# Attention of later blocks: two 64-row chunks in nine visits inside y, instead of one chunk in 17 visits between h and y

## The chip, the cores and the metric

The kernel runs on one core of a Trainium2 chip. The metric is the device time of one execution in microseconds (us), of which the median over several runs is given. TensorE (PE) multiplies, VectorE (DVE), ScalarE (ACT) and GpSimd (POOL) work element by element, and SyncE (SP) issues the DMAs, which are the loads and stores between the chip's main memory and the on-chip buffers. Each engine executes its own instructions in order, and waits at an instruction until what it needs is there.

## The reference

A linear attention with decay works on blocks of 64 rows and carries a 64x64 state for each of 2 x 8 heads over the 12 blocks of a sequence. Its output goes through two MLPs, one after the other.

```python
# q, k, v: (2, 8, 768, 64); lam: (8,), between 0.97 and 0.99
for b in range(12):
    qb, kb, vb = the 64 rows of block b
    intra = (qb @ kb.T * Dmask) @ vb            # Dmask[i, j] = lam ** (i - j) for i >= j
    inter = (qb * lam ** (pos + 1)) @ kv_state
    out[block b] = intra + inter
    kv_state = lam ** 64 * kv_state + (kb * lam ** (63 - pos)).T @ vb
x = out as (1536, 512)
h = x @ w_in;  g = where(h > 0, h, exp(min(h, 0)) - 1);  x = g @ w_out      # 512 -> 2048 -> 512
h = x @ w_in2; g = P(h) / Q(h), a cubic over 1 + |b0 h| + |b1| h * h;  y = g @ w_out2
```

## The kernel before

The 1536 tokens are three blocks t of T = 512. Each MLP layer takes a block in NF = 16 steps f of 128 hidden units: `mlp_h` is the product x @ w_in of step f, 12 matmuls of 512 columns (line 435), and `mlp_y` adds g @ w_out into four accumulating banks, 12 matmuls (line 517, and line 426 for a block's last y). There are 12 since every operand is split into a high and a low part in a narrower float type, and three of the four products are computed for each of four tiles. y runs LAG = 2 steps behind h. Between them stand, for each step, relu and exp on ScalarE (lines 448 and 449), max on VectorE (line 450, which frees h's bank), the high part ghi on ScalarE (line 452) and the low part glo on VectorE (line 453).

A first stage computes the attention of token block 0 in chunks of 128. The attention of blocks 1 and 2 is done in 64-row chunks, numbered 8 to 23, by `att_visit` in the steps of t = 0 and t = 1 of layer 0 (step s = 16 t + f). A visit stands between h and y of its step. On TensorE it has up to four matmuls of 64 x 64 for each of four pairs of heads, in two quadrants each: the scores k · q of a chunk n (line 340), and for the chunk d of the visit before scores · v (line 345), the state's product k · v (line 351) and state · q (line 356). Around them stand the fade of q by powers of lam on POOL (line 371), the mask on VectorE (line 376), the copy of d's outputs `sm_out` on ScalarE (line 384), the decay of the keys, `sm_decay_k`, on ScalarE (line 365), and the state: addition on VectorE (line 388), decay on ScalarE (line 395). The first visit also makes the powers of lam for 64 rows by four matmuls (line 333).

The order on each engine is written out by hand here (`manual_schedule`): what the program issues first stands first in an engine's queue. SP's queue is in program order through the whole kernel. It carries the loads of raw weights (lines 114 and 122), of k and q (`qk`, line 308, two DMAs) and of k and v (`kv`, line 323, four DMAs a chunk). Raw weights come as 64-bit numbers, of which VectorE makes 32-bit ones by three integer instructions (lines 78, 81 and 84); their high half is then made on ScalarE (line 127) and the low half on VectorE (line 128). During t = 1 `park_w2` does the same for half of the second layer's weights and stores them. The visits of before are at the steps f given here, for t = 0 and t = 1:

```python
visits = [(3, 5, 7, 9, 10, 12, 13, 14, 15), (2, 4, 6, 8, 10, 12, 14, 15)]
```

Of the kernel before, what the change touches and what calls it, by code (L numbers as in the profile page):

```python
# [8 lines left out]
F32 = mybir.dt.float32  # L9
# [3 lines left out]
ALU = mybir.AluOpType  # L13
# [16 lines left out]
def fused_kernel(ctx, tc, lam, qkv, w1, w2, ab, out):  # L30
# [16 lines left out]
    ph = ctx.enter_context(tc.tile_pool(name="ph", bufs=2, space=PSUM))  # L47
# [252 lines left out]
    aa_tiles = []  # L300

    def sm_load_qk(k):
# [10 lines left out]
        for b in range(2):  # L313
            chunk[k + b] = {"q": qk[:, :, 0, b * CS:(b + 1) * CS],
                            "k": qk[:, :, 1, (1 - b) * CS:(2 - b) * CS]}

    def sm_load_kv(k):
        c, b, row = k // 2, k % 2, 4 * P
        chunk[k]["kv"] = kv = qq.tile([P, NP, 2, D], F32, tag="kv", name=f"kv{k}")
# [7 lines left out]
    def sm_products(n, d):  # L327

        if not aa_tiles:
            aa_tiles.extend(pa.tile([P, T], F32, tag=f"pa{i}", name=f"aa{i}")  # L330
                            .rearrange("p (x m i) -> p x m i", x=2, m=NP) for i in range(2))
            for r in ROWS:
                nc.tensor.matmul(aa_tiles[1][r, 1], lhsT=pick[r], rhs=mask64[r, :, 1:CS + 1],  # L333
                                 start=True, stop=True, skip_group_check=True)
            nc.scalar.activation(out=qpow[:, :, 0:CS], in_=aa_tiles[1][:, 1], func=AF.Copy)
        pn, pd = chunk.get(n), chunk.get(d)
        for m in range(NP):
            if pn:
                for r in ROWS:
                    nc.tensor.matmul(aa_tiles[0][r, 0, m], lhsT=pn["k"][r, m],  # L340
                                     rhs=pn["q"][r, m], start=True, stop=True,
                                     skip_group_check=True)
            if pd:
                for i, r in enumerate(ROWS):
                    nc.tensor.matmul(aa_tiles[1][ROWS[1 - i], 0, m], lhsT=pd["kv"][r, m, 1],  # L345
                                     rhs=pd["s"][r, m], start=m == 0, stop=d % KB == 0,
                                     skip_group_check=True)
        for m in range(NP):
            if pd and d % KB < KB - 1:
                for r in ROWS:  # L350
                    nc.tensor.matmul(aa_tiles[0][r, 1, m], lhsT=pd["kv"][r, m, 0],  # L351
                                     rhs=pd["kv"][r, m, 1], start=True, stop=True,
                                     skip_group_check=True)
            if pd and d % KB:
                for i, r in enumerate(ROWS):
                    nc.tensor.matmul(aa_tiles[1][ROWS[1 - i], 0, m], lhsT=state[r, m, 0],  # L356
                                     rhs=pd["q"][r, m], start=False, stop=True,
                                     skip_group_check=True)

    def sm_decay_k(n):  # L360

        kv = chunk[n]["kv"]
        if n % KB < KB - 1:
            for m in range(NP):
                nc.scalar.activation(out=kv[:, m, 0], in_=kv[:, m, 0], func=AF.Copy,
                                     scale=mask64[:, m, CS - 1:CS])

    def sm_decay_q(n):
        q = chunk[n]["q"]
        if n % KB:  # L370
            nc.gpsimd.tensor_tensor(out=q, in0=q, in1=qpow[:, :, 0:CS], op=ALU.mult)

    def sm_mask(n):
        b = chunk[n]
        b["s"] = s = ap_.tile([P, NP, CS], F32, tag="s", name=f"s{n}")
        nc.vector.tensor_tensor(out=s, in0=aa_tiles[0][:, 0], in1=mask64[:, :, 0:CS], op=ALU.mult)

    def sm_out(d):

        t, js = d * CS // T, slice(d * CS % T, d * CS % T + CS)  # L380
        if t not in xraw:
            xraw[t] = xr.tile([P, NP, T], F32, tag="xr", name=f"xr{t}")
        first, last = d % KB == 0, d % KB == KB - 1
        nc.scalar.activation(out=xraw[t][:, :, js], in_=aa_tiles[1][:, 0], func=AF.Copy)
        if first:
            nc.scalar.activation(out=state[:, :, 0], in_=aa_tiles[0][:, 1], func=AF.Copy)
        elif not last:
            nc.vector.tensor_tensor(out=state[:, :, 0], in0=aa_tiles[0][:, 1],
                                    in1=state[:, :, 1], op=ALU.add)

    def sm_decay_state(d):

        if d % KB not in (0, KB - 1):
            for m in range(NP):
                nc.scalar.activation(out=state[:, m, 1], in_=state[:, m, 0], func=AF.Copy,
                                     scale=qpow[:, m, CS - 1:CS])

# [102 lines left out]
    def mlp_y(layer, t, f):  # L500
# [27 lines left out]
    with ExitStack() as actx:  # L528
# [4 lines left out]
        qq = actx.enter_context(tc.tile_pool(name="qq", bufs=2))  # L533

# [20 lines left out]
        dmask = ac.tile([P, H, C + 1], F32, name="dmask")  # L555
        qpow = ac.tile([P, NP, C], F32, name="qpow")
        state = ac.tile([P, NP, 2, D], F32, name="state")

        mask64 = dmask.rearrange("p (m h) i -> p m h i", h=2)[:, :, 1, CS:]
# [19 lines left out]
        yy, hh = ((py, "y"),) * 2, ((ph, "h"),) * 2  # L579
# [323 lines left out]
```

## Time and profile before

| | |
|---|---|
| median of 3 runs (lowest to highest) | 571.95 us (571.62 to 572.47) |
| profiled execution | 572.56 us |
| its span, first to last instruction | 570.8 us |
| mean granted TensorE clock | 0.999 |
| TensorE busy | 564.6 us, 99% of the span |
| VectorE busy | 464.7 us, 81% |
| ScalarE busy | 358.5 us, 63% |
| GpSimd busy | 29.8 us, 5% |
| DMA traffic | 64.58 MB, 113 GB/s in the mean |

Busy time is the time in which an engine works on an instruction; matmuls overlap one another, so TensorE's is no measure of its efficiency. The span leaves out what lies around the program; the profiled execution's own time holds it. All rows further down are from this one execution, and their times count from the span's start.

### The profile page before, as it was taken

What the parts mean: (1) busy time and instruction counts of PE and PEld (TensorE: products, weight loads), DVE (VectorE), ACT (ScalarE), POOL (GpSimd) and SP (SyncE); (2) the same over time, 40 slices, a digit from 0 to 9 for tenths busy, and PEclk for the clock granted to TensorE, in tenths of its full rate; (3) what the DMA queues carried; (4) which work ended last, traced back from release to release, by engine and by line L of the source; (5) the groups of instructions that cost most, each with busy time, mean ns of one, the idle gap of its engine ahead of it and who ended that gap; (6) DMA issues with size and microseconds to landing.
All of it is one profiled execution on the core that took longest, in us unless ns stands there. A gap on an engine that the chain in (4) does not pass through costs nothing.

```text
span 570.8 us, 9255 instructions
## 1 busy us (share of the span) xinstructions
PE 564.6 (99%) x3550; PEld 464.9 (81%) x3550; DVE 464.7 (81%) x722; ACT 358.5 (63%) x690; POOL 29.8 (5%) x51
## 2 busy tenths in 40 slices
PE   8999999999999999999999999999999999999997
PEld 7877888888888888888888888888888888888885
DVE  6999999965676635877979999888898888898882
ACT  3746646875554545555568976667877666776672
POOL 7401001100100000000000000000000000000000
PEclk9999999999999999999999999999999999999999
DMA  8977677464687513434432500000400000200001
GB/s 291 318 225 243 237 227 214 107 206 128 204 240 229 165 49 136 167 135 177 150 108 78 182 3 1 1 2 0 145 3 2 0 1 0 75 0 1 1 1 74
DMA packets 41215, 64.58 MB, mean 113 GB/s; under 512 B 20178, under 2 KB 20178, under 8 KB 41170
## 3 DMA queue, kind: packets, MB, share of 16 engines
q1 hardware_dynamic: 41168, 63.98, 35.8%
q8 instruction: 28, 0.46, 0.3%
q14 instruction: 17, 0.14, 0.1%
q10 hardware_dynamic: 2, 0.00, 0.0%
HBM read 53.48 MB, written 10.49 MB: 112 GB/s over the span
## 4 chain that ended last, share of the span: by engine, by line
PE 98%; DMA 1%; SPq 0%; ACT 0%; issue 0%
PE h L435 46%; PE y L517 43%; PE y L426 3%; PE aa L340 1%; DMA att<-qkv_in 1%; PE aa L351 1%; PE pa L243 1%; PE pa L209 1%; PE pa L249 0%; PE aa L356 0%; PE aa L345 0%; SPq L192 0%; PE sums L256 0%; PE pa L291 0%; ACT o L487 0%; PE aa L333 0%
## 5 line engine op out<-in xcount | busy, mean ns | idle before, releaser
L435 PE MATMUL h<-xhi,w 128*128 128x512 f32 x768 | 204.8, 389 | 0.0
L517 PE MATMUL y<-ghi,w 128*128 128x512 f32 x712 | 191.8, 392 | 0.0
L435 PEld LDWEIGHTS h<-xhi,w 128*128 128x128 f32 x768 | 143.8, 188 | 30.3 <-DVE w L128 0.4
L517 PEld LDWEIGHTS y<-ghi,w 128*128 128x128 f32 x712 | 132.3, 188 | 27.8
L435 PE MATMUL h<-xlo,w 128*128 128x512 f32 x384 | 102.6, 389 | 0.0
L517 PE MATMUL y<-glo,w 128*128 128x512 f32 x356 | 95.3, 389 | 0.0
L435 PEld LDWEIGHTS h<-xlo,w 128*128 128x128 f32 x384 | 72.1, 188 | 15.0
L517 PEld LDWEIGHTS y<-glo,w 128*128 128x128 f32 x356 | 66.8, 188 | 14.2
L461 ACT ACTIVATE a<-h,babs 128x512 f32<-128x512 f32 x48 | 33.0, 688 | 63.8 <-PE h L435 63.8
L448 ACT ACTIVATE a<-h 128x512 f32<-128x512 f32 x48 | 28.3, 589 | 43.1 <-PE h L435 42.9
L465 DVE SCALAR_TENSOR_TENSOR b<-b,babs,a 128x512 f32<-128x512 f32 x48 | 36.0, 751 | 20.9 <-ACT b L462 20.7
L450 DVE SCALAR_TENSOR_TENSOR b<-a,h 128x512 f32<-128x512 f32 x48 | 32.7, 681 | 15.3 <-ACT a L449 12.1
L452 ACT ACTIVATE ghi<-b 128x512 fp32r<-128x512 f32 x48 | 30.0, 626 | 22.4 <-DVE b L450 22.4
L453 DVE TENSOR_TENSOR glo<-b,ghi 128x512 fp32r<-128x512 f32 x48 | 34.0, 709 | 7.0 <-ACT ghi L452 4.8
L463 ACT ACTIVATE p<-h,cab 128x512 f32<-128x512 f32 x48 | 37.7, 785 | 0.0
L467 ACT ACTIVATE a<-b,one 128x512 f32<-128x512 f32 x48 | 35.0, 729 | 3.1 <-DVE b L465 2.6
L469 DVE SCALAR_TENSOR_TENSOR p<-p,cab,h 128x512 f32<-128x512 f32 x48 | 35.8, 746 | 1.2
L473 DVE SCALAR_TENSOR_TENSOR b<-b,one,a 128x512 f32<-128x512 f32 x48 | 35.8, 746 | 0.1
L475 DVE SCALAR_TENSOR_TENSOR p<-p,cab,a 128x512 f32<-128x512 f32 x48 | 35.8, 746 | 0.0
L58 DVE TENSOR_TENSOR glo<-p,ghi 128x512 fp32r<-128x512 f32 x48 | 33.0, 688 | 3.0 <-PE y L426 1.5
L468 DVE TENSOR_TENSOR p<-p,h 128x512 f32<-128x512 f32 x48 | 32.8, 682 | 2.9 <-ACT p L463 2.9
L477 DVE SCALAR_TENSOR_TENSOR p<-b,p 128x512 f32<-128x512 f32 x48 | 33.1, 690 | 1.2
(88 smaller groups left out, 611.2 us busy)
## 6 DMA issues: line engine op xcount, KB each, us to landing
raw<-w_in SPq DMA_DIRECT2D x64, 512.0 KB, 4.5
att<-qkv_in SPq DMA_DIRECT2D x16, 256.0 KB, 6.0
qk<-qkv_in SPq DMA_DIRECT2D x16, 256.0 KB, 4.3
kv<-qkv_in SPq DMA_DIRECT2D x64, 64.0 KB, 4.0
w2d<-wbuf SPq DMA_DIRECT2D x16, 256.0 KB, 4.5
wbuf<-w2d SPq DMA_DIRECT2D x16, 256.0 KB, 2.8
x2d<-o SPq DMA_DIRECT2D x12, 256.0 KB, 2.3
x2r<-x2d SPq DMA_DIRECT2D x12, 256.0 KB, 3.1
```

The source lines that it names most:

```text
L58: lo_eng.tensor_tensor(out=lo, in0=src, in1=hi.bitcast(F32), op=ALU.subtract)
L435: nc.tensor.matmul(h, lhsT=w[:, a, 0, k * P:(k + 1) * P], rhs=xs[layer, t, k][b], start=i == k == 0, stop=i == 2 and k == NP - 1)
L453: lambda: nc.vector.tensor_tensor(out=glo, in0=b, in1=ghi.bitcast(F32), op=ALU.subtract)]
L461: nc.scalar.activation(out=a, in_=h, func=AF.Abs, scale=babs[:, 0:1])
L463: nc.scalar.activation(out=p, in_=h, func=AF.Identity, scale=cab[:, 3:4], bias=cab[:, 2:3])
L465: nc.vector.scalar_tensor_tensor(out=b, in0=b, scalar=babs[:, 1:2], in1=a, op0=ALU.mult, op1=ALU.add)
L467: nc.scalar.activation(out=a, in_=b, func=AF.Ln, bias=one[:, 0:1])
L469: nc.vector.scalar_tensor_tensor(out=p, in0=p, scalar=cab[:, 1:2], in1=h, op0=ALU.add, op1=ALU.mult)
L473: nc.vector.scalar_tensor_tensor(out=b, in0=b, scalar=one[:, 0:1], in1=a, op0=ALU.add, op1=ALU.mult)
L475: nc.vector.scalar_tensor_tensor(out=p, in0=p, scalar=cab[:, 0:1], in1=a, op0=ALU.add, op1=ALU.mult)
L477: nc.vector.scalar_tensor_tensor(out=p, in0=b, scalar=2.0, in1=p, op0=ALU.subtract, op1=ALU.mult, reverse0=True)
L517: nc.tensor.matmul(ys[layer, t][m], lhsT=w[:, a, 1, m * P:(m + 1) * P], rhs=g[b], start=f == i == 0, stop=False)
```

## The change

Two chunks are handled in one visit, and there are nine visits instead of 17, at the steps `at = [3, 6, 9, 11, 14, 18, 22, 26, 30]`. A visit stands inside the y of its step, behind the seventh of its twelve matmuls. Its outputs go to the bank of h that is free at that time, so the two banks of h have fixed names, h0 and h1, and take turns with the step. The scores of both chunks share one bank (aa1), the state's products another (aa0); the state has three parts instead of two. The keys of a visit are decayed in the step before it, state additions and decays are in the two steps behind it. The ten DMAs of a pair (kv of an odd chunk, qk, kv of the next chunk) are issued together, at the end of the step of the visit before. The tables of masks and powers for 64 rows are made in the first stage; those for 128 rows lie in a weight's place. `load_raw(2)` is called in step 8 instead of step 3. In the steps with a visit the last of the instructions on weights is issued behind the visit.

```diff
+    def sm_products(n, d, spare):
+        if d is not None:
+            aa_x[0] = spare.rearrange("p (m x i) -> p m x i", x=2, m=NP)
+        for j in range(2):
+            pn = chunk.get(n + j) if n is not None else None
+            pd = chunk.get(d + j) if d is not None else None
+            for m in range(NP):
+                if pn: ...   # scores of n + j into aa_tiles[1][r, j, m]
+                if pd: ...   # scores . v of d + j into aa_x[0][., m, j]
+        for j in range(2):
+            c = n + j - 1 if n is not None else None
+            kv = chunk[c]["kv"] if c in chunk and c % KB < KB - 1 else None
+            pd = chunk.get(d + j) if d is not None and (d + j) % KB else None
+            for m in range(NP):
+                if kv is not None: ...   # k . v of chunk c into aa_tiles[0][r, j, m]
+                if pd: ...   # state j . q of d + j into aa_x[0][., m, j]
...
     def sm_decay_q(n):
-        q = chunk[n]["q"]
-        if n % KB:
-            nc.gpsimd.tensor_tensor(out=q, in0=q, in1=qpow[:, :, 0:CS], op=ALU.mult)
+        q = chunk[n]["qk"][:, :, 0].rearrange("p m (b i) -> p m b i", b=2)
+        nc.gpsimd.tensor_tensor(
+            out=q, in0=q, in1=pow64.rearrange("p m (b i) -> p m b i", b=1)
+            .to_broadcast([P, NP, 2, CS]), op=ALU.mult)
...
-    def mlp_y(layer, t, f):
+    def mlp_y(layer, t, f, between=None):
...
+                if between and (i, m) == (1, 2):
+                    between()
...
+        at = [3, 6, 9, 11, 14, NF + 2, NF + 6, NF + 10, NF + 14]
+        pairs = list(range(first, end, 2))
+        loads = {}
+        for i, k in enumerate(pairs[1:]):
+            for j, load in enumerate(((sm_load_kv, k - 1), (sm_load_qk, k), (sm_load_kv, k))):
+                loads.setdefault(at[i] if i else 1 + j, []).append(load)
+        loads.setdefault(at[-2], []).append((sm_load_kv, end - 1))
+        work, late, states = {}, {}, {}
+        for v, s in enumerate(at[:-1]):
+            k = first + 2 * v
+            if v:
+                late.setdefault(s - 1, []).extend((sm_decay_k, n) for n in (k - 1, k))
+            work.setdefault(s + 1, []).append((sm_decay_state, k))
+            states[s + 1] = k + 1
+            work.setdefault(s + 2 + (s + 2 == NF), []).append((sm_decay_state, k + 1))
...
+        def att_visit(s, f):
+            v = at.index(s)
+            spare = ph.tile([P, T], F32, tag=f"h{(f + 1) % 2}", name=f"ax{s}") if v else None
+            n = pairs[v] if v < len(pairs) else None
+            d = pairs[v - 1] if v else None
+            sm_products(n, d, spare)
+            if d is not None:
+                sm_out(d)
             if n is not None:
                 sm_mask(n)
                 sm_decay_q(n)
...
-                if t == 0 and f == 3:
+                if t == 0 and f == 8:
                     load_raw(2)
+                if len(queue) > LAG:
+                    mlp_y(*queue.pop(0), between=(lambda: att_visit(s, f)) if s in at else None)
+                if s in at:
+                    for w in now:
+                        run(w, 1)
                 lows = [op for w in now for op in w]
-                if len(queue) > LAG:
-                    mlp_y(*queue.pop(0))
+                for load, k in loads.get(s, ()):
+                    load(k)
```

ScalarE's queue in steps 10 and 11 of before, from the exp of step 10 to the high halves of step 11's weights; `a_0_10` is step 10's buffer, `kv_1051` a chunk's keys and values, `xr` the block's attention outputs, `ghi_0_10` the high part of g:

```order
L449 ACTIVATE a_0_10_1083<-a_0_10_1083 128x512
L384 ACTIVATE xr_763<-aa_613 128x4x64
L365 ACTIVATE kv_1051<-kv_1051,dmask 128x64 x4
L127 ACTIVATE w_10_1088<-wbuf 128x512 x2
L452 ACTIVATE ghi_0_10_1081<-b_0_10_1084 128x512
L448 ACTIVATE a_0_11_1170<-h_0_11_1155 128x512
L449 ACTIVATE a_0_11_1170<-a_0_11_1170 128x512
L127 ACTIVATE w_11_1182<-wbuf 128x1024
```

The same place in the changed kernel, where line 375 is the decay of the keys, 405 and 414 are the state's copy and its decay, and line 397 is `sm_out` of the visit at step 11:

```order
L467 ACTIVATE a_0_10_1143<-a_0_10_1143 128x512
L405 ACTIVATE state<-aa_462 128x4x64
L375 ACTIVATE kv_1115<-kv_1115,mask_162 128x64 x4
L375 ACTIVATE kv_1123<-kv_1123,mask_162 128x64 x4
L127 ACTIVATE w_10_1148<-wbuf 128x512 x2
L470 ACTIVATE ghi_0_10_1141<-b_0_10_1144 128x512
L414 ACTIVATE state<-state,pow_163 128x64 x4
L466 ACTIVATE a_0_11_1200<-h_0_11_1185 128x512
L467 ACTIVATE a_0_11_1200<-a_0_11_1200 128x512
L397 ACTIVATE xr_884<-ax_1226 128x4x128
L127 ACTIVATE w_11_1293<-wbuf 128x1024
```

Two chunks' keys stand there instead of one, ahead of the weights, and `sm_out` has moved behind step 11's exp.

SP's queue of before from the raw weights of step 9 to those of step 13 (`raw_12` are the raw weights of step 12, `kv` and `qk` chunks):

```order
L122 DMA raw_9_911<-w_in 128x1024 x2
L323 DMA kv_914<-qkv_in 64x4x64 x4
L308 DMA qk_919<-qkv_in 64x2x512 x2
L122 DMA raw_11_967<-w_in 128x1024 x2
L122 DMA raw_12_1048<-w_in 128x1024 x2
L323 DMA kv_1051<-qkv_in 64x4x64 x4
L114 DMA raw_14_1_1131<-w_in 128x1024
L114 DMA raw_15_1_1133<-w_in 128x1024
L323 DMA kv_1135<-qkv_in 64x4x64 x4
L308 DMA qk_1140<-qkv_in 64x2x512 x2
L122 DMA raw_13_1184<-w_in 128x1024 x2
```

And in the changed kernel:

```order
L122 DMA raw_9_943<-w_in 128x1024 x2
L122 DMA raw_11_991<-w_in 128x1024 x2
L114 DMA raw_12_0_994<-w_in 128x1024
L114 DMA raw_10_1_996<-w_in 128x1024
L122 DMA raw_12_1038<-w_in 128x1024 x2
L323 DMA kv_1115<-qkv_in 64x4x64 x4
L308 DMA qk_1120<-qkv_in 64x2x512 x2
L323 DMA kv_1123<-qkv_in 64x4x64 x4
L114 DMA raw_14_1_1169<-w_in 128x1024
L114 DMA raw_15_1_1171<-w_in 128x1024
L122 DMA raw_13_1216<-w_in 128x1024 x2
```

The loads of the pair for the visit at step 11 stand in one group behind the raw weights of step 12; `raw_12_0` and `raw_10_1` are the raw halves that moved to step 8.

VectorE's queue at the end of t = 1 in before; `b_1_15` is the max of the last step of the block, `xlo_2` the third block's low part, `raw_0_0` the first raw half of the second layer:

```order
L450 SCALAR_TENSOR_TENSOR b_1_14_2479<-a_1_14_2478,h_1_14_2463 128x512
L453 TENSOR_TENSOR glo_1_14_2477<-b_1_14_2479,ghi_1_14_2476 128x512
L58 TENSOR_TENSOR xlo_2_0_2598<-xr_1715,xhi_2_0_2597 128x512 x2
L58 TENSOR_TENSOR xlo_2_1_2604<-xr_1715,xhi_2_1_2603 128x512 x2
L450 SCALAR_TENSOR_TENSOR b_1_15_2550<-a_1_15_2549,h_1_15_2534 128x512
L78 TENSOR_SCALAR wbuf<-raw_0_0_2627 128x512
```

And in the changed kernel:

```order
L468 SCALAR_TENSOR_TENSOR b_1_14_2481<-a_1_14_2480,h_1_14_2465 128x512
L471 TENSOR_TENSOR glo_1_14_2479<-b_1_14_2481,ghi_1_14_2478 128x512
L78 TENSOR_SCALAR wbuf<-raw_0_0_2610 128x512
L81 SCALAR_TENSOR_TENSOR wbuf<-raw_0_0_2610,wbuf 128x512
L84 SCALAR_TENSOR_TENSOR wbuf<-raw_0_0_2610,wbuf 128x512
L78 TENSOR_SCALAR wbuf<-raw_0_1_2612 128x512
L81 SCALAR_TENSOR_TENSOR wbuf<-raw_0_1_2612,wbuf 128x512
L58 TENSOR_TENSOR xlo_2_0_2580<-xr_1784,xhi_2_0_2579 128x512 x2
L58 TENSOR_TENSOR xlo_2_1_2586<-xr_1784,xhi_2_1_2585 128x512 x2
L468 SCALAR_TENSOR_TENSOR b_1_15_2549<-a_1_15_2548,h_1_15_2533 128x512
```

Five instructions on the second layer's raw weights stand ahead of xlo and of the last max, where before they stood behind.

## Rows read from the trace of the kernel before

**Rows 1.** The page: shares of the chain that ended last, by engine.

```profile
PE 98%; DMA 1%; SPq 0%; ACT 0%; issue 0%
```

**Rows 2.** Chain of waits, 57 to 70 us: start us, us, engine, tile, line, count.

```profile
57.47 2.72 PE h L435 x12
...
60.41 0.04 PE aa L340 x2
...
61.23 0.04 PE aa L351 x2
61.28 2.95 PE y L517 x12
```

**Rows 3.** Chain of waits, 33 to 57 us.

```profile
35.58 0.58 PE aa L333 x4
...
45.01 2.95 PE h L435 x12
...
52.03 2.72 PE h L435 x12
```

**Rows 4.** VectorE's timeline, 30 to 96 us: start, us, instruction, [idle before <-releaser].

```profile
40.05 1.70 DVE L81 SCALAR_TENSOR_TENSOR w<-raw,w 128x1024 int32<-128x1024 int32 x1
...
44.88 0.70 DVE L78 TENSOR_SCALAR w<-raw 128x1024 int32<-128x1024 int32 x1 [1.26 <-DMA raw<-w_in]
...
52.58 0.42 DVE L376 TENSOR_TENSOR s<-aa,dmask 128x256 f32<-128x256 f32 x1
...
55.64 0.68 DVE L450 SCALAR_TENSOR_TENSOR b<-a,h 128x512 f32<-128x512 f32 x1
...
77.77 1.23 DVE L84 SCALAR_TENSOR_TENSOR w<-raw,w 128x1024 int32<-128x1024 int32 x1
```

**Rows 5.** SP's timeline, 74 to 110 us: start, time of the issues, DMA.

```profile
79.02 0.80 SPq L122 DMA_DIRECT2D raw<-w_in  x2
79.94 2.52 SPq L323 DMA_DIRECT2D kv<-qkv_in  x4
...
88.80 1.26 SPq L308 DMA_DIRECT2D qk<-qkv_in  x2
```

**Rows 6.** DMA issues, 79 to 92 us: KB each, median us to landing.

```profile
kv<-qkv_in SPq DMA_DIRECT2D x8, 64.0 KB, 4.0
```

**Rows 7.** ScalarE's timeline, 72 to 96 us.

```profile
84.91 1.07 ACT L365 ACTIVATE kv<-kv,dmask 128x64 f32<-128x64 f32 x4 [2.88 <-DMA kv<-qkv_in]
85.88 1.14 ACT L127 ACTIVATE w<-wbuf 128x512 fp32r<-128x512 f32 x2
86.92 0.62 ACT L452 ACTIVATE ghi<-b 128x512 fp32r<-128x512 f32 x1
87.44 0.58 ACT L448 ACTIVATE a<-h 128x512 f32<-128x512 f32 x1
88.05 0.63 ACT L449 ACTIVATE a<-a 128x512 f32<-128x512 f32 x1
...
94.21 0.37 ACT L384 ACTIVATE xr<-aa 128x256 f32<-128x256 f32 x1
```

**Rows 8.** Chain of waits, 70 to 98 us.

```profile
76.43 2.72 PE h L435 x12
```

**Rows 9.** Line 371 (POOL) and line 81 (VectorE): ns min/median/max, first to last.

```profile
L371 POOL TENSOR_TENSOR qk<-qk,qpow x15: 732/737/1643, 39.9 to 203.2; 128x256 f32<-128x256 f32 x15
L81 DVE SCALAR_TENSOR_TENSOR w<-raw,w x10: 1209/1218/1704, 23.4 to 76.5; 128x1024 int32<-128x1024 int32 x10
```

**Rows 10.** Chain of waits, 205 to 225 us.

```profile
210.30 5.67 PE y L517 x24
```

**Rows 11.** VectorE's timeline, 198 to 216 us.

```profile
211.48 2.50 DVE L58 TENSOR_TENSOR xlo<-xr,xhi 128x512 fp32r<-128x512 f32 x4 [5.16 <-ACT xhi L57]
```

**Rows 12.** The raw weights, 209 to 216 us: two loads.

```profile
DMA to landing us min/median/max: 4.6/5.0/5.5
```

More of the change, by code (lines that the diff above doesn't have):

```diff
@@ L325, in sm_load_kv @@
                     [[row, CS], [P, 4], [1, D]]))
[L327 to L358, printed above, removed]
@@ L360, in sm_decay_k @@
     def sm_decay_k(n):
-        kv = chunk[n]["kv"]
-        if n % KB < KB - 1:
+        if n in chunk and n % KB < KB - 1:
+            kv = chunk[n]["kv"]
             for m in range(NP):
@@ L376, in sm_mask @@
[L376 removed]
+        s = ap_.tile([P, 2, NP, CS], F32, tag="s", name=f"s{n}")
+        for j in range(2):
+            chunk[n + j]["s"] = s[:, j]
+        nc.vector.tensor_tensor(
+            out=s, in0=aa_tiles[1], in1=mask64[:, :, 0:CS].rearrange("p (b m) i -> p b m i", b=1)
+            .to_broadcast([P, 2, NP, CS]), op=ALU.mult)
     def sm_out(d):
[L380 removed]
+        t, js = d * CS // T, slice(d * CS % T, d * CS % T + 2 * CS)
@@ L391, in sm_decay_state, with sm_state @@
-    def sm_decay_state(d):
-        if d % KB not in (0, KB - 1):
+        nc.scalar.activation(out=xraw[t][:, :, js].rearrange("p m (b i) -> p m b i", b=2),
+                             in_=aa_x[0], func=AF.Copy)
+    def sm_state(n):
+        if n - 1 in chunk and n % KB:
+            j = n % 2
+            if n % KB == 1:
+                nc.scalar.activation(out=state[:, :, j], in_=aa_tiles[0][:, j], func=AF.Copy)
+            else:
+                nc.vector.tensor_tensor(out=state[:, :, j], in0=aa_tiles[0][:, j],
+                                        in1=state[:, :, 2], op=ALU.add)
@@ L584, in fused_kernel @@
         first, end = todo[0], todo[-1] + 1
-        loads = [[(sm_load_qk, first), (sm_load_kv, first)], [(sm_load_kv, first + 1)],
-                 [(sm_load_qk, first + 2)]]
-        loads += [[(sm_load_kv, k + 1)] + [(sm_load_qk, k + 2)] * (k % 2 == 0 and k + 2 < end)
-                  for k in range(first + 1, end - 1)]
+        at = [3, 6, 9, 11, 14, NF + 2, NF + 6, NF + 10, NF + 14]
[13 more added lines that the diff above has]
+            work.setdefault(s + 2 + (s + 2 == NF), []).append((sm_decay_state, k + 1))
         with tc.manual_schedule():
@@ L606, in fused_kernel @@
             load_pair(1)
-            for load, k in loads.pop(0):
-                load(k)
+            for load in (sm_load_qk, sm_load_kv):
+                load(first)
             def s_part(i):
@@ L667, in fused_kernel @@
             low(2)
+            for i, r in enumerate(ROWS):
+                nc.gpsimd.tensor_copy(
+                    out=mask64[r], in_=dmask.rearrange("p (m h) i -> p m h i", h=2)
+                    [r, :, 1 - i, (1 - i) * CS:(1 - i) * CS + CS + 1])
             s_part(4)
@@ L711, in fused_kernel @@
         queue = []
-        def att_visit(due, more):
-            n = todo.pop(0) if more and todo else None
-            d = due.pop() if due else None
-            sm_products(n, d)
+        def att_visit(s, f):
[6 more added lines that the diff above has]
+                sm_out(d)
             if n is not None:
@@ L720, in att_visit @@
                 sm_decay_q(n)
-                due.append(n)
             if d is not None:
-                sm_out(d)
-                del chunk[d]
+                if n is not None:
+                    sm_state(n)
+                for j in range(2):
+                    del chunk[d + j]
         with tc.manual_schedule():
-            due = []
-            next_d = []
             lows = w
@@ L777, in fused_kernel @@
                     att_hand(*atts[-1])
-                if f in visits[t]:
-                    att_visit(due, t == 0 or f < NF - 1)
-                    next_d = list(due)
-                    for n in due:
-                        if f < NF - 1:
-                            sm_decay_k(n)
+                    aa_tiles.append(pa.tile([P, T], F32, tag="pa0", name="aa0")
+                                    .rearrange("p (x m i) -> p x m i", x=2, m=NP))
+                    sm_decay_k(first)
+                if s in states:
+                    sm_state(states[s])
+                for op, n in late.get(s, ()):
+                    op(n)
                 for w in now if t or f else ():
-                    run(w, len(w) - 1)
+                    run(w, len(w) - (2 if s in at else 1))
                 if t == 0 and f + 2 < FULL:
```

86 lines of the change are left out of this document (51 added, 35 removed).

## The prediction

> **What bounds the kernel now.** I read the share line of the chain first: TensorE carries 98% of it and DMA 1%, so a microsecond counts only where it reaches TensorE [rows 1]. Next I read the chain stretch by stretch, as the list of what TensorE does in one step. Twelve MLP matmuls take 2.72 us, and a step without a visit is h and y, 5.44 us [rows 3]. A step with a visit runs from 57.47 to the end of the y at 61.28 + 2.95 = 64.23, 6.76 us, so the visit costs 1.32 us [rows 2]. Inside it, from 60.41 to 61.23 the reader sees fourteen of its 16 pairs of quadrant matmuls, 0.82 us or 0.0587 us a pair; sixteen make 0.94, which leaves 0.38 a visit that doesn't depend on its size; 0.23 of that is the y behind it, 2.95 instead of 2.72. Then I read the other engines' rows for those that arrive just in time, since the change ties TensorE to them at new places: VectorE from 45 to 79 us (its wait on a raw weight, 1.26 us) [rows 4], the loads that SP issues from 79 us [rows 5, 6], and ScalarE, where a decay of keys waited 2.88 us for its load with everything behind it in order [rows 7].
>
> **Visits.** Removed are 17 visits: the first about 1.28 us (its powers, 0.58 us in the chain, and 0.46 of scores and the rest) and sixteen of at most 1.32 (a last one lacks the scores; I leave that out), together 1.28 + 16 × 1.32 = 22.4 us. Added are nine. A pair visit with all its four kinds has 32 pair steps: 32 × 0.0587 + 0.38 = 2.26 us; the first (no outputs yet) counts 24: 1.79 us. 1.79 + 8 × 2.26 = 19.87, so 2.54 us are saved. The four matmuls of the powers come back in the first stage, where I take 0.44 of their 0.58 us [rows 3]; the bounds are 0 (the stage waits there for something else) and 0.6. In step 5 the chain has 2.95 us for an h of 2.72 [rows 3], because late weights held it up; the shift by 0.44 and the missing visit hide that: −0.25. TensorE's own part is −2.54 + 0.44 − 0.25 = −2.35 us. If the switch into and out of the small matmuls inside y costs twice (y is cut in two), 0.23 × 8 = 1.8 us of that are lost; by the row the second price is paid once per visit, so I keep −2.35.
>
> **The wait at the visits for a bank.** Each visit from step 6 on writes the bank that h(s−1) filled, so it waits until max(s−1) on VectorE has read that. In step 6 the first seven matmuls of y are through at 52.03 + 2.72 + 7 × 0.227 = 56.34 us before [rows 3]; without the visit at 5 (1.32) and the wait (0.25), with the powers (0.44) and a first visit longer by 0.51, at 55.7. VectorE is back to back from 44.88 us, where the raw weights land, to the max at 55.64 + 0.68 = 56.32 [rows 4]. One of its two attention instructions of 0.42 us (0.33 when they overlap) goes from that stretch: 56.0. That is a wait of 0.3 us; 0 if the load lands 0.3 earlier, 1.0 if both stay in the stretch and the longer mask of the first visit, 128x512, delays it further. I take 0.3. Behind the visit in TensorE's queue stand five matmuls of y and the next h; all of it shifts. At 9 and 11 VectorE has the same work with more TensorE time between, and at 14 and in block 1 it idles, so I take 0.
>
> **The wait behind the visit at 11.** This is the largest term. The next h that takes the bank must wait for sm_out, the copy on ScalarE. The loads of the pair that is due at 11 go out at the end of step 9, behind the raw weights that SP issues at 79.02, when the third instruction of narrowing (77.77 + 1.23) has freed their place [rows 4, 5]. At SP's pace (kv 2.52 us, qk 1.26) the order is kv 79.9 to 82.5, qk to 83.8, the second kv from 83.85 to 86.35. Before, the group issued at 79.94 let ScalarE start at 84.91, 4.97 us later [rows 5, 7]; that gives 88.8 for the second kv, a little less without a raw pair right ahead of it: 88.5. By the median from issue to landing, 4.0 us [rows 6], the last of its four (issued 85.75) lands at 89.7, and the early end is 87.5. ScalarE's queue holds, behind those decays: the high halves of weights (2), ghi, four decays of the state, relu, exp, and then sm_out. From start to start in the rows that is 0.97 + 1.04 + 0.52 + 0.97 (as the other decays) + 0.61 + 0.54 [rows 7], and sm_out of twice the old 0.37's size, 0.55: 5.2 us. So sm_out ends at 93.7. On TensorE, step 10's h starts at 76.43 before [rows 8]; three pair visits (6.31 us) instead of the first and three single ones (5.24), the powers, the wait gone and that of step 6 make it 78.0. Step 11 starts 5.44 later at 83.4, its y at 86.15, the visit stands from 87.75 to 90.0, the rest of y to 91.35. The h of step 12 is due then and stands for 93.7 − 91.35 = 2.35 us; with the landings of 87.5 and 89.7 it is 1.35 to 3.55, and with the whole wait hidden 0. I take 2.4. In the kernel before the same late load cost nothing, since only h's own chain stood behind it.
>
> The Trainium skill ("DMA: Bandwidth & Descriptors", Anatomy of one DMA — SWDGE (gpsimd) path) puts one DMA at about 2.0 us fixed and the rest by bytes at 436 GB/s, which is 2.15 us for a kv load of 64 KB. The trace doesn't agree, with a median of 4.0 us beside other loads [rows 6]. By the page the last kv would land at 87.9 and this term would be 1.8 us, the sum 0.6 lower; I go by the row.
>
> **The last bank.** In front of the third block h takes the bank of h(31), so max(31) has to be through. VectorE now narrows one and two thirds raw halves before xlo and max(31). Counted from the end E of the last visit, h(32) is due at 1.36 + 3 × 2.72 = E + 9.52 (before, the two y stood there as 5.67 us [rows 10]). The raw halves are issued right behind the visit and took 4.6 and 5.5 us to land [rows 12]; narrowing 1.1 us of the second from E + 6.0 or so, xlo 2.50 [rows 11] and max 0.6 end at E + 9.3 to E + 10.8, the early end with landings of some 4 us. That is 0 to 1.35 us; I take 0.5.
>
> **What else moves.** The POOL fade takes in two chunks; mostly it took 0.74 us, its longest 1.64. The first began at 39.9, and the L81 of VectorE at 40.05 beside it took 1.70 instead of 1.22 us [rows 4, 9]. So the doubled fade may cost VectorE 0 to 0.5 us more by step 9; with it SP's issue at 79.02 and the stall at 12 come later by as much. I take 0, since one mask and one state instruction of VectorE fall away there too. The Trainium skill ("GPSIMD Engine Reference", 1. Specifications) says that GpSimd shares its SBUF interfaces with VectorE and contends with VectorE instructions that have two SBUF inputs. The trace agrees (the 1.70 against 1.22); that speaks against the change by up to those 0.5 us. Decays of keys a step ahead are the same number of ScalarE instructions, which idles; their cost is the term at 11. Raw halves at step 8 instead of 3 take two loads out of a busy stretch and pass no load that is waited for: 0, at most 0.2 either way. The two POOL copies of the mask lie in a wait of the first stage. Later parks and the block's start: 0 to 0.4, at 0.
>
> **The sum.** −2.35 + 0.3 + 2.4 + 0.5 = +0.85 us. The profiled execution took 572.56 us (570.8 in the span), so 573.4 by its measure; it stands 0.6 us above the median of the runs, 571.95, and against that the forecast is 572.8. This is within 0.2% (1.14 us, about what a measurement of this kernel can tell from no change). With each term at its ends: −2.6 to −0.5, 0 to 1.0, 1.35 to 3.55, 0 to 1.35; not all at once, so 571.8 to 574.0 for this case.
>
> **Rivals.**
> - *The waits stay hidden.* The loads land by 86 us, or ScalarE is ahead, and only TensorE's saving is seen, with 0 to 0.5 us for the rest: 571.95 − 2.35 + 0.5 = 570.1, between 569.6 and 570.9. For it: ScalarE's wait of 2.88 us for the same kind of load reached TensorE nowhere. Against it: the 4.97 us, and ScalarE's order. Chance 0.21.
> - *Slower, by late loads at step 9.* The load that VectorE waited for before 44.88 was late in a crowded stretch too; if the second kv takes 7 us here instead of 4.65, ScalarE starts its decays at 83.85 + 7.05 = 90.9 instead of 88.5, and the stall is 4.8 instead of 2.4 us: 575.2. It decides from a landing 0.3 us behind my 88.5, where the sum passes +1.14. For it: the raw weights, two qk and kv pieces go out in one run of ten issues. Against it: the median of 4.0 us in just this stretch. Chance 0.14.
> - *A pair saves nothing.* What is left over a visit, 0.38 us, belongs to each chunk and not to each visit (the small matmuls drain at each change of target bank): then 2.54 us are not saved, and the waits are still there, partly hidden by longer visits: 571.95 + 0.85 + 2.54 − 0.8 = 574.5, where 0.8 is the part of the stall at 12 that two longer visits cover. For it: the 0.38 is a remainder. Against it: 0.23 of it is seen in the y behind the visit. Chance 0.08.
>
> **How the numbers follow.** The forecast's case has 0.57. Below 570.8 lies most of the first rival: faster 0.19. Over 573.1 lie both slower rivals and a third of the forecast's case: 0.22 + 0.19 = 0.41. The rest, 0.40, is no change. The range leaves out the lowest tenth in the first rival and the highest in the second: 570.3 to 574.9.
>
> **What would show it.** In the profile after: pair visits of some 2.26 us and y of 2.95 around them; h of step 12 released by ScalarE's copy of two chunks after a wait of 1 to 4 us; ScalarE idle on a kv load from some 82 to 88.5; a short wait of the visit at 6 for the max; the h of the third block's start held by VectorE. I am wrong if the h of step 12 doesn't wait, or if pair visits take 1.9 or 2.6 us.

## The result and the profile after

The changed kernel takes 577.91 us in the median of 6 runs (576.99 to 579.04), the kernel before 572.00 beside it: 1.0103 times as long (95% interval 1.0092 to 1.0113), 5.9 us slower. The forecast was 572.8 with a range of 570.3 to 574.9, so the kernel is slower than the whole range allows. The profiled execution took 577.87 us with a span of 576.1.

The chain's share line no longer has TensorE alone (the page of the changed kernel, shares by engine; it answers to [rows 1]):

```profile
PE 85%; DVE 5%; DMA 4%; ACT 3%; issue 1%; SPq 1%; DVEq 0%; ACTq 0%
```

Where the time went is found by measuring each step, from the first matmul of its h to that of the next, in both traces. Without a visit a step is 5.44 us in both; steps 16 and 32, the first of a block, hold h alone and are 2.72, and 15 and 31, the last, hold a second y and are 8.16. These are the steps that differ, with what is left when the work of the visit itself (1.32 before, 2.25 after) is taken off:

| step | before, us | after, us | left over in after |
|---|---|---|---|
| 3, first visit | 6.73 | 7.21 | 0 |
| 5 | 7.03 | 5.48 | 0 |
| 6 | 5.44 | 8.13 | 0.44 |
| 7, 10, 13, 20, 24, 28 | 6.76 each | 5.44 to 5.45 each | 0 |
| 9, 14, 22, 26, 30 | 6.76 each | 7.68 to 7.71 each | 0 |
| 11 | 5.44 | 12.97 | 5.28 |
| 12 | 6.75 | 5.57 | 0.13 |
| 15, 31 | 9.48, 9.47 | 8.16 each | 0 |
| 16 | 2.72 | 3.58 | 0.86 |
| 18 | 6.76 | 8.78 | 1.09 |
| 32 | 2.72 | 3.11 | 0.39 |

The nine visits make 1.77 + 8 × 2.25 = 19.8 us against 22.4 before, which is the saving that was forecast. The left-over waits sum to 8.2 us. At the h of step 33 the changed kernel is 5.57 us late: 0.15 from the start, −2.6 for the visits, −0.27 for step 5, 8.2 for the waits, and 0.1 in pieces under 0.05. What follows gives back 0.24 of it, so the spans differ by 5.3.

The visit at 22 as the chain of waits has it (start us, us, what; it answers to [rows 2]): y is cut at 160.00 + 1.59 and goes on at 163.61, 2.02 us of small matmuls between, and 0.23 more about the seam.

```profile
157.28 2.72 PE h L453 x12
160.00 1.59 PE y L535 x7
...
163.61 1.36 PE y L535 x5
164.97 2.72 PE h L453 x12
```

Step 11 is the main loss. SP's timeline of the changed kernel, 66 to 112 us (start, time of the issues, DMA; it answers to [rows 5]):

```profile
80.63 0.81 SPq L122 DMA_DIRECT2D raw<-w_in  x2
81.53 2.51 SPq L323 DMA_DIRECT2D kv<-qkv_in  x4
84.15 1.26 SPq L308 DMA_DIRECT2D qk<-qkv_in  x2
85.45 2.57 SPq L323 DMA_DIRECT2D kv<-qkv_in  x4
```

ScalarE's timeline in the same stretch ([rows 7]):

```profile
87.05 1.06 ACT L375 ACTIVATE kv<-kv,mask 128x64 f32<-128x64 f32 x4 [3.16 <-DMA kv<-qkv_in]
90.82 1.06 ACT L375 ACTIVATE kv<-kv,mask 128x64 f32<-128x64 f32 x4 [2.71 <-DMA kv<-qkv_in]
91.79 1.13 ACT L127 ACTIVATE w<-wbuf 128x512 fp32r<-128x512 f32 x2
92.83 0.61 ACT L470 ACTIVATE ghi<-b 128x512 fp32r<-128x512 f32 x1
93.35 1.05 ACT L414 ACTIVATE state<-state,pow 128x64 f32<-128x64 f32 x4
94.31 0.58 ACT L466 ACTIVATE a<-h 128x512 f32<-128x512 f32 x1
94.91 0.63 ACT L467 ACTIVATE a<-a 128x512 f32<-128x512 f32 x1
95.45 0.58 ACT L397 ACTIVATE xr<-ax 128x512 f32<-128x512 f32 x1
```

And what TensorE waited for from 80 to 98 us (us in total, times, longest):

```profile
PE aa L346 <- DMA qk<-qkv_in: 2.0, 2, 1.1
PE h L453 <- ACT xr L397: 1.2, 1, 1.2
```

The reader sees one late group of loads twice. The visit itself, due after the seventh matmul, waits 2.0 us for qk. Behind these waits TensorE's granted clock falls to 0.50, the lower of its two levels (1.2 GHz), from 90.1 to 93.5 us, and the visit's small matmuls run in that stretch. By an estimate, half of 3.4 us, that is 1.7 more; in all the visit is 3.9 us too long. One window of it (us, busy times of the engines as PE, PEld, DVE, ACT, POOL, then the granted clock, DMA share, GB/s):

```profile
91.00:93.00 2.00, 2.00 (x73) 2.00 (x69) 0.56 (x1) 2.00 (x7) 1.07 (x1) 0.50 0.78 309
```

Then h waits for the copy of the visit's outputs, which stands behind the decays, the weights, ghi, the state and step 11's relu and exp in ScalarE's queue: another 1.4. It is this second wait that sets the time. From the second kv on (90.82) ScalarE works without a pause up to the copy (95.45), 2 us behind the visit's end, so a faster visit would have changed nothing here; nor is the one execution with a mean clock of 1.000 (577.78) any faster than the others at 0.996 and 0.997 (576.99 to 579.04).

The group goes out 1.6 us later than before (80.63 against 79.02 [rows 5]). VectorE releases the raw weights ahead of it, and this is VectorE there (start, us, instruction; it answers to the last of [rows 4]):

```profile
76.42 1.78 DVE L471 TENSOR_TENSOR glo<-b,ghi 128x512 fp32r<-128x512 f32 x1
78.13 1.21 DVE L81 SCALAR_TENSOR_TENSOR w<-raw,w 128x1024 int32<-128x1024 int32 x1
79.38 1.23 DVE L84 SCALAR_TENSOR_TENSOR w<-raw,w 128x1024 int32<-128x1024 int32 x1
```

A glo that elsewhere takes 0.69 us takes 1.78. On POOL the fade, now of 128x512, runs beside it:

```profile
75.67 1.98 POOL L380 TENSOR_TENSOR qk<-qk,pow 128x512 f32<-128x512 f32 x1 [16.87 <-PE ax L351]
```

The same stands at steps 3 and 6, where the glos at 39.38 and 57.58 take 1.78 us too. In all three the glo ends 0.55 us behind the fade's end (78.20 and 77.65 here).

### The profile page after: what moved, and what is told of

Read it like the earlier page. It is cut to its first block, busy times and chain, and to the rows that moved or that the text cites. A ratio compares the mean times of both kernels' runs of the same rounds, so it can differ in the third digit from the quotient of the medians.

```text
span 576.1 us, 9237 instructions
## 1 busy us (share of the span) xinstructions
PE 568.0 (99%) x3550; PEld 467.8 (81%) x3550; DVE 467.6 (81%) x714; ACT 358.2 (62%) x682; POOL 29.4 (5%) x45
## 4 chain that ended last, share of the span: by engine, by line
PE 85%; DVE 5%; DMA 4%; ACT 3%; issue 1%; SPq 1%; DVEq 0%; ACTq 0%
PE h L453 40%; PE y L535 36%; PE y L444 3%; DMA raw<-w_in 2%; DMA kv<-qkv_in 1%; DVE glo L471 1%; PE pa L209 1%; DVE w L81 1%; PE pa L243 1%; SPq L323 1%; ACT w L127 1%; DVE w L84 1%; DVE w L128 1%; PE ax L351 1%; ACT state L414 1%
## 5 line engine op out<-in xcount | busy, mean ns | idle before, releaser
L535 PE MATMUL y<-glo,w 128*128 128x512 f32 x356 | 97.6, 392 | 0.0
L471 DVE TENSOR_TENSOR glo<-b,ghi 128x512 fp32r<-128x512 f32 x48 | 36.2, 756 | 9.2 <-ACT ghi L470 8.3
```

The costliest lines, as they stand in the source:

```text
L471: lambda: nc.vector.tensor_tensor(out=glo, in0=b, in1=ghi.bitcast(F32), op=ALU.subtract)]
```

## The experiments

Ratios are to the kernel before, run beside each one; the changed kernel itself is 1.0103. All but the last four are the changed kernel with one edit. A trace is one execution, and the total is the median of several.

**The loads first.**

```diff
-                    load_pair(... FULL - 1: (FULL + 2, NF - 4) ...)    # in step 9, ahead of the visit
                 for load, k in loads.get(s, ()):
                     load(k)
+                if s == FULL - 1:
+                    load_pair(FULL + 2, NF - 4)
```

> Only edit to the changed kernel (577.9 us): at the end of step 9 the ten DMAs of the pair for the visit at 11 are issued ahead of the raw weights of step 12, not behind them. Theory A (the 5.3 us that step 11 is too long are the late second kv load plus ScalarE's order behind it): the issues start at the end of the visit at 9, some 4 us earlier, the second kv lands by 86.5 instead of 91.0, the stall of the h of step 12 falls from 5.3 (with the visit's own wait) to under 1, total 573.2 (572.6 to 574.0). Rival B (VectorE is late anyway, by its contention with the fade on POOL, and would hold the visit or the weights of step 12): the stall stays at 3 or more, now with VectorE as its releaser, total 576 to 577.

574.88 us, ratio 1.0047 (1.0033 to 1.0060). SP issues the first kv at 75.18, the second at 80.80. Step 11 takes 9.55 us: 3.4 of the 5.28 us go, the visit waits for nothing, and 1.86 stay, all at ScalarE's copy, since the second kv still comes at 87.06 and the same queue stands behind it:

```profile
87.06 1.07 ACT L375 ACTIVATE kv<-kv,mask 128x64 f32<-128x64 f32 x4 [1.51 <-DMA kv<-qkv_in]
```

Theory A is right in kind, but the total lies above its range: the loads landed later than it said, as the issues took 9.7 us from first to last instead of 6.5, and the order on ScalarE kept 1.86.

**Nearly no fade on POOL.** It fades 4 of 64 columns and leaves out the rest of the fade, so its outputs are not the kernel's.

```diff
-        q = chunk[n]["qk"][:, :, 0].rearrange("p m (b i) -> p m b i", b=2)
+        q = chunk[n]["qk"][:, :, 0].rearrange("p m (b i) -> p m b i", b=2)[:, :, :, 0:4]
```

> Leaves out most of the fade of q by powers on POOL (4 of 64 columns of each chunk are faded), everything else as in the changed kernel (577.9 us). Contention theory: the glo of VectorE that takes 1.78 instead of 0.69 us behind the fades at the visits of steps 6 and 9 goes back to 0.69, the third narrowing instruction of step 9 ends at 79.5 instead of 80.6, the raw weights, kv and ScalarE's decays behind it come 1.1 us earlier, step 11 is shorter by 1.1 to 1.6; total 576.3 to 576.8. Rival (the long glo has another cause, and the loads' own time alone makes the stall): glo stays at 1.78, total 577.7 to 578.0.

576.12 us, ratio 1.0064 (1.0047 to 1.0081). VectorE at the same place:

```profile
75.08 0.68 DVE L471 TENSOR_TENSOR glo<-b,ghi 128x512 fp32r<-128x512 f32 x1
75.69 1.27 DVE L81 SCALAR_TENSOR_TENSOR w<-raw,w 128x1024 int32<-128x1024 int32 x1
76.99 1.22 DVE L84 SCALAR_TENSOR_TENSOR w<-raw,w 128x1024 int32<-128x1024 int32 x1
```

glo is back at 0.68, the narrowing ends 2.4 us earlier (78.2 against 80.6), step 11 takes 11.05 (−1.9), and the wait of step 16 is gone (2.72). The traced execution is the shortest of five, 574.37 us at a mean granted clock of 1.000, and the other four took 576.03 to 576.62 at 0.997 to 0.999; so the gain in the median is 1.8 us, not the trace's 3.5. The contention is shown: the fade is charged to VectorE, and by way of VectorE to the loads.

**The output copies first.**

```diff
-                for op, n in late.get(s, ()):
+                for op, n in late.get(s, ()) if s != NF + 1 else ():
                     op(n)
...   # behind mlp_y
+                for op, n in late.get(s, ()) if s == NF + 1 else ():
+                    op(n)
```

> Only edit to the changed kernel (577.9 us): in step 17 ScalarE's eight decays of keys for the visit at 18 stand behind the four copies of the first block's outputs instead of ahead of them. Theory: the copies start 2 us earlier, the first y of block 1 no longer waits for them bank by bank (0.8 us), and the stores and the max that waits for a store come earlier (0.25 us at the visit): step 18 goes from 8.8 to 7.7 us, total 576.8. Rival: the decays, now behind the copies, hold the visit at 18 for as long: step 18 stays within 0.3, total 577.6 to 577.9.

576.90 us, ratio 1.0082 (1.0068 to 1.0097), as forecast. Step 18 goes from 8.78 to 7.69. In this trace steps 6, 11 and 16 are 1.3 shorter together and step 26 is 1.0 longer as well, which the forecast did not have. ScalarE in the changed kernel, and then here:

```profile
132.11 2.01 ACT L375 ACTIVATE kv<-kv,mask 128x64 f32<-128x64 f32 x8
134.02 2.02 ACT L505 ACTIVATE o<-y 128x512 f32<-128x512 f32 x4
```

```profile
130.73 2.04 ACT L505 ACTIVATE o<-y 128x512 f32<-128x512 f32 x4
132.64 2.03 ACT L375 ACTIVATE kv<-kv,mask 128x64 f32<-128x64 f32 x8
```

y of block 1 needs the four banks that the copies empty from 134.87 on in the one, so it ran bank by bank behind them.

**Another bank.**

```diff
-    nh = [0]
+    nh = [1]
```

> Only edit to the changed kernel (577.9 us): the first h of the third block takes bank pa0 and not that of the h just before it; the rotation of four banks goes on from there. Theory: its wait for VectorE's max of step 31 (the start of step 32 is 0.39 us late) goes, total 577.5. Rival: xlo, which VectorE makes in the same stretch, holds it as long, total 577.9.

577.11 us, ratio 1.0088 (1.0069 to 1.0108); the step is 2.72 instead of 3.11 us, as forecast. The trace shows a wait of 0.5 us for a glo in step 26 instead, behind a weight that VectorE could not write before an earlier store (1.6 us); the run of the output copies has a longer step 26, too (8.67, with the same wait of 0.7), and three others one longer by 0.2 to 0.3. It comes and goes between runs.

**Visits at 12 and 15.**

```diff
-        at = [3, 6, 9, 11, 14, NF + 2, NF + 6, NF + 10, NF + 14]
+        at = [3, 6, 9, 12, 15, NF + 2, NF + 6, NF + 10, NF + 14]
```

> Only edit to the changed kernel (577.9 us): the visits at steps 11 and 14 move to 12 and 15, so there are three steps from one visit and its loads to the next one throughout block 0. Theory A (the 5.3 us of step 11 are the loads of a pair that have two steps, of which the order of SP and ScalarE leave too little): the wait goes, since the decays stand one step later and the load is there by then; step 12 takes 7.7 to 8.3 us and step 11 5.4; total 572.4 to 573.5. Rival B (VectorE's own lateness, by the fades on POOL, is what holds the visit): 2 us or more of the wait move to the visit at 12, total 575 to 576. The waits at steps 16 and 18 (0.9 and 1.1) can come or go by a few tenths with the visit at 15.

572.74 us, ratio 1.0004 (0.9994 to 1.0015). Steps 11 and 12 take 5.44 and 7.68: nothing is left of the wait, though VectorE and the fade are as they were, and the second kv is issued at 84.91. Two numbers of the table are worth 5.2 us, nearly all of it by the first, since step 14 had no wait to lose. Theory A holds; what VectorE loses to the fade reaches this visit only where its loads have two steps instead of three.

**Decays at 11.**

```diff
-                late.setdefault(s - 1, []).extend(...)
+                late.setdefault(s - (s != 11), []).extend(...)
```

> Only edit to the changed kernel (577.9 us): the keys for the visit at 11 are decayed in step 11, behind its relu and exp, not a step ahead. The load lands as late as before (91.0 us), but nothing of step 10 stands behind it on ScalarE. Theory: of the 5.3 us the part that the order on ScalarE makes goes: the visit ends 1 us behind the last decay at 92, its copy follows at once, the h of step 12 comes at about 94.2 instead of 96.15; step 11 takes 11.0 instead of 13.0, total 575.9. Rival (the landing alone sets it): step 11 stays within 0.5 of 13.0, total 577.5 to 578. Other rival (the order makes all of it): step 11 under 8.5, total 573.5.

574.76 us, ratio 1.0044 (1.0026 to 1.0061). Step 11 takes 10.61 us (2.9 left, all in the visit; the copy no longer holds h), and step 16 takes 2.72. So of the 5.28 us the order on ScalarE makes about 2.4 and the loads' lateness 2.9. The 0.86 of step 16 and 0.7 of step 18 are gone as well, as with nearly no fade; how they hang on step 11 is not shown.

**Raw halves at step 3.**

```diff
-                if t == 0 and f == 8:
+                if t == 0 and f == 3:
```

> Only edit to the changed kernel (577.9 us): the two raw halves are loaded in step 3 again, not in step 8. Theory: they are no part of the loss; without them at 74.6 us the raw weights and the kv behind them land at most 0.3 earlier, and the loads of step 4 land a little later; total 577.4 to 578.2. Rival (their traffic makes the kv for the visit at 11 late): step 11 takes 12.0 or less, total under 577.

578.78 us, 0.6 above its forecast; the ratio of 1.0102 (1.0088 to 1.0117) is the changed kernel's own. Steps 7 to 9 are 1.2 us longer in its profile (one h waits 0.4 us for ScalarE's high weights) and step 11 0.3 shorter. No part of the loss.

**The fade on VectorE.**

```diff
-        nc.gpsimd.tensor_tensor(
+        nc.vector.tensor_tensor(
             out=q, in0=q, in1=pow64...
```

> Only edit to the changed kernel (577.9 us): the fade of q of both chunks runs on VectorE and not on POOL. It does all the work, so VectorE has some 0.6 us more in each of eight visits. Contention theory: the fade on POOL costs VectorE 1.1 us at each of the visits at 6 and 9, more than the fade itself; the third narrowing of step 9 ends about 1.0 us earlier, at 79.6, and step 11 takes 12.0 instead of 13.0 us, total 576.5 to 577.2. Rival (VectorE's own work counts like contention): step 11 takes 13 or more, total 577.9 to 579.

578.34 us, ratio 1.0102 (1.0084 to 1.0121): a miss in the total. glo takes 0.69 and the narrowing ends at 79.71, 0.9 earlier as forecast, so a fade of 0.68 on VectorE costs it less than one of 1.98 on POOL. But step 6 grows by 0.8, step 11 falls by 0.5 only, since SP's issue of the raw weights ahead of the group takes 1.50 us instead of 0.81 and the second kv goes out just 0.2 earlier (85.25), and step 12 grows by 1.6. There the granted clock is 0.50 again, behind a wait of h for the copy of 2.4 us (same columns as at step 11):

```profile
97.00:100.00 3.00, 3.00 (x8) 2.32 (x7) 3.00 (x6) 1.17 (x2) 0.00 (x0) 0.50 0.36 132
```

Here nothing hides the low clock. The one execution with a mean clock of 1.000 took 576.63 us, as forecast; of the five at 0.996 or 0.997 one took 576.71 and four 578.31 or more. So the clock is seen to make step 12 longer, but that it is the whole miss is not shown. Steps 16 and 18 are 0.9 and 0.7 shorter.

**The visit ahead of y.**

```diff
+        if between:
+            between()
         for i, (a, b) in enumerate(PARTS):
...
-                if between and (i, m) == (1, 2):
-                    between()
```

> Only edit to the changed kernel (577.9 us): each visit stands ahead of its step's y and not behind the seventh of its matmuls, 1.59 us earlier. It writes the bank whose max ends on VectorE 1.5 to 2 us behind the end of h in the steps where VectorE has no slack. Theory: the visits at 6, 9 and 14 wait 1 to 2 us each, the others less, and at 11 nothing changes since the loads set it; total 580 to 583. Rival: the max has long been done, total within 0.5 of 577.9, so the place inside y saves nothing.

578.89 us, ratio 1.0117 (1.0102 to 1.0132), between the two. The visit at 6 waits for the max, as the theory said:

```profile
PE ax L351 <- DVE b L468: 1.9, 1, 1.9
```

Steps 6, 14 and 18 are 1.8, 1.0 and 0.9 longer; 9, 22, 26 and 30 are the same; 11 is 1.8 and 16 0.9 shorter. At step 11 that is TensorE coming later to loads that are no later: the h of step 12 starts at 95.98 us here and at 96.08 in the changed kernel. The place inside y is worth having, though the wait at 11 hides most of it here.

**The kernel before once more.**

> The kernel before, once more, for its first stage: in nine traces of changed kernels, all with the same first stage, the first h starts between 21.3 and 23.1 us, in the one trace of the kernel before at 21.0. If loads at the start set this time, it differs by tenths here too (21.0 to 22.5), and the powers' four matmuls cost less than the spread; if the matmuls of the powers set it, it is 21.0 again.

Its first h starts at 21.01 us in the chain, against 21.11 in the first trace, and its step 5 takes 6.76: the chain has 2.72 us for that h where [rows 3] have 2.95.

```profile
44.90 2.72 PE h L435 x12
```

At step 33 it is 0.38 ahead of the first trace, 0.27 of it by step 5; so the 0.25 of step 5 was one execution's, no gain of the change. The start is 21.0 again, as it is to be if the powers set it; 21.0 is also the low end of the other theory's range. In the changed kernel's chain the four matmuls of the powers stand right ahead of the first h:

```profile
20.68 0.58 PE aa L332 x4
```

They are 0.58 us there, against 0.44 forecast; but what stands ahead of them was 0.3 to 0.4 earlier than in the two traces of before, and the first h of the nine traces of changed kernels starts at 21.26 to 22.52. A difference of starts alone can't give the powers' price.

**Three of them together**: visits at 12 and 15, copies first, other bank.

> The visits at 12 and 15, the decays of step 17 behind the output copies, and the other bank for the first h of block 2, all in one: each takes away a wait that the trace of the changed kernel shows (5.3, about 1.0, 0.4). If the waits are the whole loss and TensorE's saving of some 2.7 us is real, the sum is 577.9 - 5.3 - 1.0 - 0.4 = 571.2, and 570.3 if the start of block 1 (0.9) goes too: a little faster than the kernel before (572.1). If the waits only move on, 573 or more.

571.82 us, ratio 0.9991 (0.9980 to 1.0002): no difference from before that can be told, and 0.6 above the 571.2 of the sum. The three waits are gone, and 0.85 us are left in step 16 (3.57).

**The split first.** The same, and:

```diff
-                if s in at:
+                if s in at and s != NF - 1:
                     for w in now:
                         run(w, 1)
```

> The kernel of the run before it (visits at 12 and 15, decays of step 17 behind the output copies, other bank; 571.8 us), and in step 15 the high half of the last weights is made behind the split of block 1's inputs, no longer ahead of it. In that kernel the weights waited 1.8 us for VectorE, which the fade on POOL had slowed (a glo of 1.77), and the split's four high parts behind them held the h of step 16 by 0.85 us. Theory: step 16 goes from 3.6 to 2.7 us, total 571.0, faster than the kernel before (572.2) by about 0.2%. Rival (the low parts, VectorE's, hold it next): step 16 stays over 3.2, total 571.6.

572.74 us, ratio 1.0010 (0.9998 to 1.0022): a miss. Step 16 falls to 3.16, but step 17 grows to 7.23, because VectorE now stands for the high half with a glo behind it, for which y waits:

```profile
121.76 0.69 DVE L128 TENSOR_TENSOR w<-wbuf,w 128x512 fp32r<-128x512 f32 x1 [2.18 <-ACT w L127]
```

**The visit of step 15 finished later.** The three together, and:

```diff
+            if s == NF - 1:
+                kept.append(lambda: finish(nc.vector))   # mask, fade on VectorE, state
+            else:
+                finish()
...
                         x_split(0, t, m)
+                    run(lows, 1)                          # high half of the last weights
+                    kept.pop(0)()
```

> The kernel with visits at 12 and 15, decays of step 17 behind the output copies and the other bank (571.8 us), and at the visit of step 15 alone: mask, fade and state addition come behind the split of block 1's inputs, the fade on VectorE, and the high half of the last weights directly behind the split's high parts. Theory (the 0.85 us that step 16 waits there are the fade on POOL, which makes a glo of VectorE 1.77 us long, with the weights, ScalarE and the split behind it): glo takes 0.69, step 16 goes from 3.57 to 2.72 us and step 17 stays at 5.44; total 571.0, between 0.1% and 0.3% faster than the kernel before. Rival (whatever comes last there holds h, the lateness being VectorE's whole work in block 0): step 16 or 17 stays 0.4 or more too long, total 571.5 or more.

570.23 us, ratio 0.9968 (0.9955 to 0.9980): faster than both kernels. VectorE in the three together, and here:

```profile
113.83 1.77 DVE L471 TENSOR_TENSOR glo<-b,ghi 128x512 fp32r<-128x512 f32 x1
```

```profile
113.26 0.68 DVE L471 TENSOR_TENSOR glo<-b,ghi 128x512 fp32r<-128x512 f32 x1
```

Steps 16 and 17 take 2.72 and 5.44. Against the kernel before, the gain over the three together is 1.3 us, of which step 16 makes 0.85; the first h of this trace also starts 0.9 earlier, and the rest isn't traced further. Since fade, mask and order were moved at once, the run shows that the wait is gone, not how much of it is the fade's; that the fade makes the 1.77 is shown by the runs with nearly no fade and with the fade on VectorE, where no glo takes over 0.74.

## Why the prediction was wrong

By the spans, 5.33 us were added and 0.85 forecast. Of the 4.5 that are missing, the wait behind the visit at 11 makes 2.9 and the start of block 1 1.95; the rest, each off by 0.3 at most, gives 0.4 back.

- *Visits: right.* 2.26 us forecast for a pair, 2.25 measured; the saving of 2.54 is 2.6. The rival of a pair that saves nothing is out. In step 5 the gain of 0.25 was no gain of the change, though this pair of traces shows it.
- *The bank at 6: right in kind, its size by luck.* 0.3 forecast, 0.44 in this trace; of the ten other traces with the same visit, seven have nothing and three 0.1 to 0.23.
- *The visit at 11: the step that failed.* Place, mechanism and queue are as forecast, and ScalarE's chain from the second kv to the end of the copy was forecast at 5.2 us and took 5.2 (90.82 to 96.03). What failed is its start, 90.82 and not 88.5, and the h that was due at 90.8 and not 91.35: 5.28 us instead of 2.4. Of the h's 0.55, 0.23 were counted twice, once in the visit's 2.26 and once in the rest of y; between the parts of y the visit takes 2.02. The start is late by 1.6 us in the issue and by 0.7 in the landing (5.37 us from 85.45 instead of 4.65), whose cause stays open. The issue's 1.6 was offered as a bound of 0.5 in "what else moves" and set to 0: the fades made a glo 1.1 longer each time, where "one mask and one state instruction of VectorE fall away there too" was to pay for it, and with nearly no fade the issue came 2.4 us earlier. The Trainium skill ("GPSIMD Engine Reference", 1. Specifications) had it: GpSimd shares its SBUF interfaces with VectorE. I had the row that bore it out (1.70 against 1.22 [rows 4, 9]) and priced a doubled instruction by no more than what the single one had cost there (0.5). The visit itself, the group's first victim, was taken as on time (87.75 to 90.0) and ended at 93.4.
- *The start of block 1: left out.* "Later parks and the block's start: 0 to 0.4, at 0" measured 0.86 + 1.09. Eight decays ahead of the output copies are 2.0 us of ScalarE in front of four banks that the next y needs; the rows for it (decays of four, 1.07 us) were there. The run with the copies first shows this 1.09. The 0.86 is gone where the fade is off POOL or nearly left out, but also with the decays at 11 and the visit ahead of y, where the fade is as it was: its cause is shown only in part.
- *The last bank: right.* 0.5 forecast, 0.39 measured, gone in all four runs with the other bank; with the same bank it is 0.03 to 0.67.
- *The rivals.* The slower one by late loads, at 0.14 and 575.2, was nearest: its place and releaser are what the trace shows, its cause (a second kv of 7.05 us) is not, for the loads were issued late and this one took 5.37. That its 90.9 for ScalarE's start is so near the 90.82 is luck. The rival of hidden waits gave 570.1, and the last run takes 570.2; that is another kernel, in which the waits were taken out and not hidden, so the agreement is no proof of the sum.

## What to carry to other kernels

When work is batched, write down for each group of loads the instruction that releases it, on which engine, and what that engine loses to the same batch; here the doubled fade delayed the engine that released the loads of the batch. An in-order queue hands one late load to everything behind it: here decays issued a step ahead of their visit cost 5 us where the loads had two steps to come, and nothing where they had three. At a block boundary list what needs the engine at once (output copies, input splits) and put prepared-ahead work behind it.

## What was not expected of the hardware

An elementwise instruction of VectorE beside one of POOL of 128x512 took 1.78 us instead of 0.69 (glo) and, in another place, the narrowing instruction with one input 1.39 instead of 0.42; POOL's own took 1.28 to 2.08. In the 7 us from 87 to 94, in which TensorE waited longest in the changed kernel, the granted clock was 0.76 in the mean: 0.50 (1.2 GHz) from 90.1 to 93.5 and 1.00 (2.4 GHz) around it. Whether that costs time depends on what ends last: in the changed kernel it lies under ScalarE's queue, in the run with the fade on VectorE it made step 12 1.6 us longer (columns as above):

```profile
87.00:94.00 7.00, 4.98 (x117) 4.24 (x116) 2.18 (x4) 4.24 (x14) 1.28 (x1) 0.76 0.88 228
94.00:97.00 3.00, 1.79 (x8) 1.16 (x7) 2.93 (x5) 2.00 (x5) 0.00 (x0) 1.00 0.00 0
```
